# Parts of four units' w_in blocks made in the second block from kept 32-bit values, instead of stored in the first

## The chip, the cores and the metric

The kernel runs on one NeuronCore of one Trainium2 chip. The metric is device time in microseconds (us) of one launch. The kernel before took 808.64 us (median of three runs, 805.9 to 810.67).

## What is computed

Chunked attention over 8 batches, 8 heads, 576 positions in chunks of 64, then a feed-forward layer over the 4608 tokens:

```python
out = softmax(q_c @ k_c.T / 8) @ v_c      # in each chunk of 64
x   = out.transpose(0, 2, 1, 3).reshape(4608, 512)
h   = x @ w_in                            # 512 x 2048
g   = h * tanh(softplus(h))
y   = g @ w_out                           # 2048 x 512
```

Results are 32-bit; each factor of the feed-forward products is split into a high part (rounded to the format that TensorE multiplies in one pass) and a low rest, and three products of the parts are added.

## The kernel before

Tokens go in blocks of 512. The first block is multiplied plainly, with w_in loaded, decoded from 64-bit patterns and split on the way. The later blocks use a seven-product scheme for 2 x 2 blocks (as Strassen's), for which w_in's 256 x 256 blocks and sums of them are needed as split operands. `ops_of[u]` is a DRAM tile with seven such operands for each of eight units u (a unit is 256 columns of w_in): slots 0 to 2 are the plain blocks A11, A12, A22, slots 3 to 6 the four sums. Each slot is 256 KB.

**Who fills the slots.** In the first block, `w_hi` (ScalarE, ACT) and `w_lo` (VectorE, DVE) split a block into `wi[u]`; `w_keep(u)` (L177 to L180) then stores slots 0, 1 and 2 from `wi[u]`, by two DMAs of 512 and 256 KB, for all eight units. The exact 32-bit values of every unit are also kept in DRAM in `cs_u` (`w_c`, L146). The sums are built later from these: `s_load` (L191 to L199) brings `cs_u` back into a buffer with 4 blocks x 2 slots x 256 values per partition, whole values in slot 1; `s_adds` (L201 to L211) makes four sums in place on DVE, 128x256 each; `s_hi` (L215, ACT) writes their high parts into slot 0 of all four blocks; `s_lo` (L219, DVE) makes the low rests and issues one 1 MB store to slots 3 to 6 (L222).

**The order.** The first block's order is the string ORDER; `keep`, `s_load`, `s_adds`, `s_hi`, `s_lo` stand in it for units 0 to 3. The second block (m = 1, about 120 to 252 us of the span, then its second phase) runs `unit(1, u)` for u = 0 to 7. A unit has seven products (n = 0 to 6) of six matmuls, each with one operand from DRAM (`load_op`, L837, five operands ahead, five buffers), between which matmuls of the unit before are put (`filled`). `beside(n)` runs after product n - 1 what BUILDS lists for (u, n). A product's PSUM bank is read by ACT or DVE before it is written again: product 3 (`v`) takes the bank of product 1 (`y`), which DVE's add at L862 reads; product 5 adds to the bank of product 4 (`x`), which ACT copies at L964; product 6 adds to the bank of product 3, which DVE adds to `zb` at L862. In units 1, 3, 5 and 7 a group of four attention tiles also passes through DVE and ACT (L324, L336, L345, L391 to L398). Units 4 to 7 have their sums built one unit ahead: adds at (u-1, 2), high at (u-1, 3), low and store at (u-1, 4), the load of the next at (u-1, 7).

**Queues.** All these loads and stores are issued by one queue, SyncE's (SP), in program order. An instruction there that waits holds up what stands behind it. `zb_p` has two buffers; one holds `wst`, then `a_both` (units 1 and 2), then `zb_1_4`, which unit 4 writes first after its product 2.

Of the kernel before, what the change touches and what calls it, by code (L numbers as in the profile page):

```python
# [9 lines left out]
F32 = mybir.dt.float32  # L10
F32R = mybir.dt.float32r
# [4 lines left out]
ALU = mybir.AluOpType  # L16
AX = mybir.AxisListType

P = 128
# [5 lines left out]
def kernel(  # L25
# [22 lines left out]
    nc = tc.nc  # L48
    NT, _, H, D = q.shape
    NF, _, DM = w_out.shape  # L50
# [3 lines left out]
    NU = NF // 2  # L54
# [5 lines left out]
    at = ctx.enter_context(tc.tile_pool(name="at", bufs=3))  # L60
# [14 lines left out]
    zb_p = ctx.enter_context(tc.tile_pool(name="zb", bufs=2))  # L75
# [5 lines left out]
    ops_of = [dram.tile([P, 7, 2, 256], F32, name=f"wa_{u}") for u in range(NU)]  # L81
# [107 lines left out]
    bld = {}  # L189

    def s_load(u):  # L191
        if u >= NU:
            return
        if u == 1:
            both = zb_p.tile([P, 2, 4, 2, 256], F32, name="a_both", tag="z")
            bld[1], bld[2] = both[:, 0], both[:, 1]
        elif u != 2:
            bld[u] = c_p.tile([P, 4, 2, 256], F32, name=f"a_{u}", tag="c")
        nc.sync.dma_start(  # L199
            out=bld[u][:, :, 1], in_=w_c[u].rearrange("p h (a c) -> p (h a) c", a=2)  # L200
        )  # L201
# [11 lines left out]
    def s_hi(u):  # L213
        t = bld[u]
        nc.scalar.copy(out=t[:, :, 0].bitcast(F32R), in_=t[:, :, 1])  # L215

    def s_lo(u):
        t = bld[u]
        nc.vector.tensor_tensor(  # L219
            out=t[:, :, 1].bitcast(F32R), in0=t[:, :, 1], in1=t[:, :, 0], op=ALU.subtract  # L220
        )
        nc.sync.dma_start(out=ops_of[u][:, 3:], in_=t)  # L222


    def t_whole(u):
# [41 lines left out]
    st = {}  # L267
# [290 lines left out]
    fill = []  # L558
# [64 lines left out]
    def run(plan_, key):  # L623
        for step, arg in plan_.get(key, ()):
            step(arg)
# [26 lines left out]
    def open_accumulators():  # L652
# [53 lines left out]
        15, exp 2, bits 15, load 17, gh 10, scale 16, inverse 2, norm 2, T 2, load_qk 3, up  # L706
        12, bits 16, hi 15, mish 11, lo 15, copy 2, gl 10, x 0 0, hi 16, scale 17, x 0 3, x
        0 4, load 18, V 2, raw 2, lo 16, bits 17, mish 12, fill 11, x 0 2, scores 3, up 13,
        max 3, gh 12, gh 11, x 0 5, gl 11, sub 3, keep 6, scale 18, bits 18, hi 17, lo 17,
        gl 12, hi 18, up 14, lo 18, exp 3, x 0 1, load_v 3, mish 13, mish 14, x 0 6, fill  # L710
        12, inverse 3, keep 5, norm 3, fill 13, keep 7, gh 13, gl 13, up 15, fill 14, s_load
        0, s_adds 0, T 3, s_load 1, ops 2, x 0 8, mish 15, gh 14, gl 14, s_hi 0, copy 3,
        keep 4, s_lo 0, s_adds 1, fl 0, gh 15, s_load 2, ops 3, x 1 0, x 0 7, gl 15, fl 1,
        at 0, x 1 1, V 3, raw 3, x 1 3, fill 15, x 1 4, x 1 2, x 1 5, at 1, x 0 9, x 1 9, x
        1 7, load_qk 4, fl 2, fl 3, x 1 8, s_hi 1, fl 4, at 2, fl 5, fl 6, at 3, x 1 6, s_lo
        1, x 0 10, x 1 10, at 4, s_load 3, at 5, fl 7, st 0, at 6, at 7, st 1, at 8, at 9,
        s_adds 2, s_hi 2, at 10, at 11, s_adds 3, s_lo 2, at 12, at 13, at 14, s_hi 3, s_lo
        3, at 15, at 16, at 17, at 18, at 19, at 20, at 21, at 22, at 23
    """

    BY_SCALAR = (2, 4, 6, 7, 8, 10, 12, 13, 14,)
# [1 line left out]
    def atom(name, *args):  # L723
# [11 lines left out]
        elif name in attention:  # L735
            attention[name](j)
        elif name == "up":
            up(a, last="w")
        elif name == "gh":
            g_upper(it[a], it[a]["z"], f"0_{a}", a in BY_SCALAR)  # L740
        elif name == "gl":
            g_lower(it[a], it[a]["z"], f"0_{a}")
        elif name == "fill":
            if a < NF - 1:
                filled()
            down(0, a, it[a])
        elif name == "fl":
            filled(3)
        elif name == "st":
            for t in (2 * a, 2 * a + 1):  # L750
                store("0", (0, 1), t)
        elif name == "mish":
            it[a]["z"] = z_tile(f"z_{a}")
            mish(it[a]["z"], it[a]["h"])
        elif name == "keep":
            w_keep(a)
        elif name == "x":
            x_step(1, *args)
        elif name == "ops":
            for _ in range(a):  # L760
                load_op()
        else:
            {"s_load": s_load, "s_adds": s_adds, "s_hi": s_hi, "s_lo": s_lo}[name](a)
# [19 lines left out]
    def first_block():  # L783
# [35 lines left out]
    ops = [  # L819
        (m, ops_of, u, OPS.index(n)) for m in range(1, BOTH_FROM) for u in range(NU) for n, _ in PRODUCTS  # L820
    ]
# [40 lines left out]
        nc.vector.tensor_tensor(out=z, in0=o, in1=z, op=ALU.add)  # L862

    zb = {}
    S_STEPS = (s_adds, s_adds, s_hi, s_lo, s_load)
    S_PLACES = (2, 2, 3, 4, 7)
    BUILDS = {(2, 7): [(s_load, 4)]}
    for u in range(4, NU):
        for n, (step, place) in enumerate(zip(S_STEPS, S_PLACES)):
            if n:  # L870
                BUILDS.setdefault((u - 1, place), []).append((step, u + n // 4))


    T_STEPS = (t_whole, t_sums, t_hi, t_lo)
# [20 lines left out]
    def unit(m, u):  # L895
# [8 lines left out]
        def beside(n):  # L904
            if m == 1:
                run(BUILDS, (u, n))
                for key in later.get(8 * u + n, ()):
# [520 lines left out]
```

## Time and profile before

| | |
|---|---|
| median of three runs | 808.64 us (805.9 to 810.67) |
| the profiled execution | 804.22 us, of it the span 802.4 us |
| TensorE (PE) busy in the span | 787.6 us |
| DVE, ACT busy | 547.5 us, 462.6 us |
| DMA moved | 196.12 MB, mean 244 GB/s |

The span runs from the first to the last instruction of the program on the core; the views below are all of this one execution. A wait is named by the engine that waited and by what ended it. A load's landing is when its data and its semaphore have arrived.

### The profile page before, as it was taken

The numbers are of one execution on the slowest core, as the hardware profiler recorded it, in microseconds if no ns is written. First come the engines' busy times: TensorE is split into PE (matmuls) and PEld (weight loads), VectorE is DVE, ScalarE is ACT, GpSimd is POOL, SyncE is SP. The second block draws the span as 40 slices with busy tenths as digits, with TensorE's granted clock in tenths as the row PEclk, the third lists the DMA queues.
The fourth block names the chain that finished last, engine by engine and source line by source line (L and its number), as shares of the span: only waits on it lengthen the run. The fifth ranks groups of instructions, "written<-read, shape, count | busy, mean of one in ns | idle before, by whom it ended". The sixth has DMA issues, their size and how long they took to land.

```text
span 802.4 us, 16472 instructions
## 1 busy us (share of the span) xinstructions
PE 787.6 (98%) x6394; PEld 680.7 (85%) x6394; DVE 547.5 (68%) x835; ACT 462.6 (58%) x694; POOL 0.7 (0%) x6
## 2 busy tenths in 40 slices
PE   4999999999999999999999999999999999999998
PEld 4888787788888888888999998888999988888887
DVE  6789898655656786676688945545698723338875
ACT  5998976534436445566655737566556434455443
POOL 0000000000000000000000000000000000000000
PEclk9999999999999999999999999999999999999999
DMA  9999989877685879988667797776676776766774
GB/s 339 310 327 346 344 290 303 296 229 275 199 296 165 292 249 284 344 297 268 180 179 214 208 279 241 246 253 199 173 209 184 235 219 194 193 195 187 214 193 130
DMA packets 101581, 196.12 MB, mean 244 GB/s; under 512 B 10112, under 2 KB 26496, under 8 KB 99456
## 3 DMA queue, kind: packets, MB, share of 16 engines
q1 hardware_dynamic: 100896, 194.29, 76.2%
q8 instruction: 51, 0.84, 0.4%
q10 hardware_dynamic: 608, 0.79, 0.3%
q14 instruction: 26, 0.21, 0.1%
HBM read 152.04 MB, written 42.99 MB: 243 GB/s over the span
## 4 chain that ended last, share of the span: by engine, by line
PE 96%; DVE 1%; DMA 1%; ACT 1%; issue 0%; ACTq 0%; DVEq 0%
PE x L850 22%; PE X L1279 12%; PE v L850 11%; PE Z L1279 6%; PE y L850 6%; PE o L565 6%; PE h L527 5%; PE Y L1279 3%; PE X_a L1231 3%; PE X L1231 3%; PE Z L1231 3%; PE av L298 2%; PE s L298 2%; PE pt L409 2%; PE Y L1231 1%; PE o_(1, 1)_0_2789 L565 1%
## 5 line engine op out<-in xcount | busy, mean ns | idle before, releaser
L1184 ACT CAST gh<-g 128x512 fp32r<-128x512 f32 x168 | 103.5, 621 | 93.1 <-PE X L1279 29.9
L1187 DVE TENSOR_TENSOR gl<-g,gh 128x512 fp32r<-128x512 f32 x168 | 115.2, 689 | 49.0 <-ACT gh L1184 45.3
L850 PE MATMUL x<-x_T,w 128*128 128x512 f32 x390 | 97.3, 391 | 0.0
L850 PEld LDWEIGHTS x<-x_T,w 128*128 128x128 f32 x390 | 72.6, 188 | 15.4 <-ACT zb L964 0.4
L862 DVE TENSOR_TENSOR g<-v,g 128x512 f32<-128x512 f32 x48 | 33.0, 690 | 73.2 <-ACT g L1162 41.9
L540 ACT ACTIVATE g<-g 128x512 f32<-128x512 f32 x72 | 44.9, 631 | 59.2 <-DVE g L862 58.9
L527 PE MATMUL h<-x_first,wi 128*128 128x512 f32 (+1 forms) x216 | 47.4, 371 | 1.1 <-ACT x_first L449 0.7
L850 PE MATMUL x<-x_T,late 128*128 128x512 f32 x186 | 46.0, 391 | 0.0
L527 PEld LDWEIGHTS h<-x_first,wi 128*128 128x128 f32 x216 | 36.8, 188 | 8.2 <-ACT x_first L449 0.8
L850 PEld LDWEIGHTS x<-x_T,late 128*128 128x128 f32 x186 | 34.6, 188 | 7.0
L1279 PE MATMUL X<-w,gh 128*128 128x256 f32 x288 | 40.5, 283 | 0.0
L565 PE MATMUL o<-wo,gh 128*128 128x512 f32 x128 | 39.5, 390 | 0.0
L1279 PEld LDWEIGHTS X<-w,gh 128*128 128x128 f32 x288 | 37.2, 192 | 0.1
L862 DVE TENSOR_TENSOR g<-y,g 128x512 f32<-128x512 f32 x24 | 16.3, 680 | 30.2 <-PE y L850 29.6
L1162 ACT COPY g<-x 128x512 f32<-128x512 f32 x24 | 14.1, 589 | 37.2 <-PE x L850 37.2
L850 PE MATMUL v<-x_B,w 128*128 128x512 f32 x138 | 35.3, 395 | 0.1
L850 PE MATMUL y<-x_B,w 128*128 128x512 f32 x126 | 31.8, 395 | 0.0
L850 PE MATMUL x<-x_B,w 128*128 128x512 f32 x126 | 31.6, 393 | 0.0
L1279 PE MATMUL X<-late,gh 128*128 128x256 f32 x224 | 31.5, 283 | 0.0
L850 PEld LDWEIGHTS v<-x_B,w 128*128 128x128 f32 x138 | 25.4, 188 | 6.2 <-DVE zb L862 1.0
L850 PE MATMUL v<-x_T,w 128*128 128x512 f32 x120 | 29.6, 390 | 0.0
L1279 PEld LDWEIGHTS X<-late,gh 128*128 128x128 f32 x224 | 28.9, 192 | 0.1
(217 smaller groups left out, 1736.0 us busy)
## 6 DMA issues: line engine op xcount, KB each, us to landing
w<-wa SPq DMA_DIRECT2D x150, 256.0 KB, 3.8
w<-wb SPq DMA_DIRECT2D x94, 256.0 KB, 2.9
late<-wa SPq DMA_DIRECT2D x74, 256.0 KB, 3.1
late<-wb SPq DMA_DIRECT2D x74, 256.0 KB, 2.9
wst<-in_w_in SPq DMA_DIRECT2D x16, 512.0 KB, 5.7
wst<-in_w_out SPq DMA_DIRECT2D x16, 512.0 KB, 6.0
v<-in_v SPq DMA_DIRECT2D x16, 512.0 KB, 6.4
wa<-a SPq DMA_DIRECT2D x6, 1024.0 KB, 4.4
```

The lines of the kernel that those rows point to most:

```text
L298: nc.tensor.matmul(o[h * CHUNK : (h + 1) * CHUNK, c, t - ts.start, g], lhsT=l[rows, t, 2 * g + h], rhs=r[rows, t, 2 * g + h], start=True, ...
L409: nc.tensor.transpose(out=d["pt", ts.start][:, t - ts.start, g], in_=d["p"][:, t, g].rearrange("p c k -> p (c k)"), identity=ident,)
L527: nc.tensor.matmul(h[:, cols], lhsT=wi[i // 2][:, i % 2 * 2 + kt // 2, w_, kt % 2], rhs=x[:, x_, kt, cols], start=(n == 0), stop=(n == 3 * ...
L540: nc.scalar.activation(out=out_, in_=in_, func=AF.Mish)
L565: nc.tensor.matmul(acc[t], lhsT=g[:, t * P : (t + 1) * P], rhs=wo[f // 2][:, f % 2, part], start=(f == 0 and n == 0), stop=(f == NF - 1 an ...
L850: nc.tensor.matmul(o, lhsT=t[:, w_, kt], rhs=x[x_][:, kt], start=(start and i == 0), stop=(i == 5), skip_group_check=not start,)
L862: nc.vector.tensor_tensor(out=z, in0=o, in1=z, op=ALU.add)
L1162: nc.scalar.copy(out=z["G22"], in_=o)
L1184: nc.scalar.copy(out=d["gh"], in_=g)
L1187: nc.vector.tensor_tensor(out=d["gl"], in0=g, in1=d["gh"].bitcast(F32), op=ALU.subtract)
L1231: nc.tensor.matmul(o, lhsT=d[g][:, t * P : (t + 1) * P], rhs=w__, start=(first and n == 2), stop=(u == NU - 1 and g == "gl"), skip_group_c ...
L1279: nc.tensor.matmul(o, lhsT=d[g][:, t * P : (t + 1) * P], rhs=w_[:, part], start=(k in (0, 1, 3) and u == 0 and t % 2 == 0 and n == 0), sto ...
```

## The change

`w_keep` is dropped for units 4 to 7 (eight DMAs, 3 MB). Slots 0 to 2 of these units are made in the second block from the values that `s_load` brings back: `kept_hi` and `kept_lo` split blocks 0 and 1 (128x512) and then block 3 (128x256), with the high and low parts put side by side in slot 0 of the buffer, and store them by two DMAs and one DMA of 256 KB. Then `s_adds`, `s_hi` and `s_lo` run as before on the same buffer; `s_hi` overwrites slot 0. Units 5 and 6 get a buffer of `zb_p` between them, and the places are a table of numbers 8u + n.

```diff
@@ s_load
-        if u == 1:
-            both = zb_p.tile([P, 2, 4, 2, 256], F32, name="a_both", tag="z")
-            bld[1], bld[2] = both[:, 0], both[:, 1]
-        elif u != 2:
+        if u in (1, 5):
+            both = zb_p.tile([P, 2, 4, 2, 256], F32, name=f"a_both_{u}", tag="z")
+            bld[u], bld[u + 1] = both[:, 0], both[:, 1]
+        elif u not in (2, 6):
             bld[u] = c_p.tile([P, 4, 2, 256], F32, name=f"a_{u}", tag="c")
...
+    def kept_slots(u, which):
+        t = bld[u]
+        if which:
+            return t[:, 3, 1], t[:, 0, 0], t[:, 1, 0]
+        return t[:, 0:2, 1], t[:, 0:2, 0], t[:, 2:4, 0]
+
+    def kept_hi(u, which):
+        whole, hi, _ = kept_slots(u, which)
+        nc.scalar.copy(out=hi.bitcast(F32R), in_=whole)
+
+    def kept_lo(u, which):
+        whole, hi, lo = kept_slots(u, which)
+        nc.vector.tensor_tensor(out=lo.bitcast(F32R), in0=whole, in1=hi, op=ALU.subtract)
+        t = bld[u][:, :, 0]
+        if which:
+            nc.sync.dma_start(out=ops_of[u][:, 2], in_=t[:, 0:2])
+        else:
+            for n in range(2):
+                nc.sync.dma_start(out=ops_of[u][:, n], in_=t[:, n::2])
...
@@ ORDER
-        max 3, gh 12, gh 11, x 0 5, gl 11, sub 3, keep 6, scale 18, bits 18, hi 17, lo 17,
+        max 3, gh 12, gh 11, x 0 5, gl 11, sub 3, scale 18, bits 18, hi 17, lo 17, gl 12, hi
...
-    S_STEPS = (s_adds, s_adds, s_hi, s_lo, s_load)
-    S_PLACES = (2, 2, 3, 4, 7)
-    BUILDS = {(2, 7): [(s_load, 4)]}
-    for u in range(4, NU):
-        for n, (step, place) in enumerate(zip(S_STEPS, S_PLACES)):
-            if n:
-                BUILDS.setdefault((u - 1, place), []).append((step, u + n // 4))
+    S_STEPS = (
+        s_load,
+        lambda u: (kept_hi(u, 0), kept_lo(u, 0)),
+        lambda u: (kept_hi(u, 1), kept_lo(u, 1)),
+        s_adds,
+        lambda u: (s_hi(u), s_lo(u)),
+    )
+    S_PLACES = {
+        4: (17, 21, 23, 24, 25),
+        5: (14, 19, 22, 27, 28),
+        6: (15, 26, 29, 30, 31),
+        7: (29, 33, 36, 40, 41),
+    }
+    BUILDS = {}
+    for u, places in S_PLACES.items():
+        for n, step in zip(places, S_STEPS):
+            BUILDS.setdefault((n // 8, n % 8), []).append((step, u))
```

In ORDER, `keep 6`, `keep 5`, `keep 7` and `keep 4` are left out and nothing else moves. PE's order is unchanged. Three places show the rest. Line numbers up to the new functions are those of before; L232, L236, L239, L242 are the new functions', and lines behind are 20 to 30 higher (L862 is L882, L837 is L857, L964 is L994).

VectorE, unit 3 up to its reciprocal, before; `a_4` is unit 4's buffer, `z_1_6<-y_1_3` the add that frees product 3's bank:

```order
L862 TENSOR_TENSOR zb_1_0_1435<-v_1_2_1872,zb_1_0_1435 128x512
L862 TENSOR_TENSOR z_1_6_1934<-y_1_3_1983,z_1_6_1934 128x512
L324 TENSOR_REDUCE m_7_0_1999<-s_7_0_1948 128x16
L336 TENSOR_TENSOR p_7_2001<-s_7_0_1948,m_7_0_1999 128x2x8x64
L211 TENSOR_TENSOR a_4_1932<-a_4_1932 128x256 x4
L551 CAST gh_1_6_2035<-z_1_6_1934 128x512
L555 TENSOR_TENSOR gl_1_6_2037<-z_1_6_1934,gh_1_6_2035 128x512
L391 TENSOR_REDUCE r_7_0_2039<-p_7_2001 128x8x2
```

The same stretch of VectorE now:

```order
L882 TENSOR_TENSOR zb_1_0_1427<-v_1_2_1873,zb_1_0_1427 128x512
L236 TENSOR_TENSOR a_4_1799<-a_4_1799 128x256
L211 TENSOR_TENSOR a_4_1799<-a_4_1799 128x256 x4
L219 TENSOR_TENSOR a_4_1799<-a_4_1799 128x4x256
L882 TENSOR_TENSOR z_1_6_1943<-y_1_3_1999,z_1_6_1943 128x512
L344 TENSOR_REDUCE m_7_0_2015<-s_7_0_1961 128x16
L356 TENSOR_TENSOR p_7_2017<-s_7_0_1961,m_7_0_2015 128x2x8x64
L236 TENSOR_TENSOR a_both_5_1751<-a_both_5_1751 128x2x256
L211 TENSOR_TENSOR a_both_5_1751<-a_both_5_1751 128x256 x4
L571 CAST gh_1_6_2054<-z_1_6_1943 128x512
L575 TENSOR_TENSOR gl_1_6_2056<-z_1_6_1943,gh_1_6_2054 128x512
L411 TENSOR_REDUCE r_7_0_2058<-p_7_2017 128x8x2
```

Unit 4's whole build (its third kept block, four adds, the low rests) stands ahead of the add that frees product 3's bank, and unit 5's first steps behind it.

ScalarE at the same place before, with the semaphores that each waits for:

```order
L924 COPY z_1_6_1934<-x_1_3_1935 128x512 [waits PE_49,Activation_49]
L540 ACTIVATE z_1_6_1934<-z_1_6_1934 128x512 [waits DVE_49]
L948 COPY zb_1_0_1435<-x_1_3_1935 128x512 [waits PE_49]
L345 ACT_TABLE_LOAD [waits DMAHW0_49]
L345 ACTIVATE p_7_2001<-p_7_2001 128x1024 [waits DVE_49]
L215 CAST a_4_1932<-a_4_1932 128x4x256 [waits DMAHW7_49,DMAHW4_49,DVE_49]
L964 COPY zb_1_0_1435<-x_1_3_1935 128x512 [waits PE_49]
```

ScalarE there now, with the semaphores that each waits for (DMAHW is a DMA's landing); L215 is `s_hi`:

```order
L232 CAST a_4_1799<-a_4_1799 128x256 [waits DMAHW2_49,Activation_49]
L954 COPY z_1_6_1943<-x_1_3_1948 128x512 [waits PE_49]
L215 CAST a_4_1799<-a_4_1799 128x4x256 [waits DMAHW3_49,DMAHW7_49,DVE_49,Activation_49]
L560 ACTIVATE z_1_6_1943<-z_1_6_1943 128x512 [waits DVE_49]
L232 CAST a_both_5_1751<-a_both_5_1751 128x2x256
L978 COPY zb_1_0_1427<-x_1_3_1948 128x512 [waits PE_49]
L365 ACT_TABLE_LOAD [waits DMAHW4_49]
L365 ACTIVATE p_7_2017<-p_7_2017 128x1024 [waits DVE_49]
L215 CAST a_both_5_1751<-a_both_5_1751 128x4x256 [waits DMAHW5_49,DVE_49]
L994 COPY zb_1_0_1427<-x_1_3_1948 128x512 [waits PE_49]
```

The L215 of `a_4` moved ahead of L345, right behind the copy of product 0's bank; in its old place stands unit 5's.

SyncE's queue at the end of unit 1 and in unit 2, before:

```order
L837 DMA w16_1738<-wa_2_110 128x512
L837 DMA w17_1755<-wa_2_110 128x512
L222 DMA wa_3_111<-a_3_1559 128x2048
L837 DMA w18_1768<-wa_2_110 128x512
L837 DMA w19_1798<-wa_2_110 128x512
L837 DMA w20_1811<-wa_2_110 128x512
L281 DMA q_7_1855<-in_q 128x2x512
L281 DMA k_7_1856<-in_k 128x2x512
L837 DMA w21_1865<-wa_3_111 128x512
```

The same stretch of the queue now; w16 to w22 are operands of products (2, 2) to (3, 1):

```order
L857 DMA w16_1730<-wa_2_110 128x512
L857 DMA w17_1747<-wa_2_110 128x512
L199 DMA a_both_5_1751<-cs_5_129 128x4x256
L222 DMA wa_3_111<-a_3_1551 128x2048
L857 DMA w18_1762<-wa_2_110 128x512
L199 DMA a_both_5_1751<-cs_6_130 128x4x256
L857 DMA w19_1793<-wa_2_110 128x512
L199 DMA a_4_1799<-cs_4_128 128x4x256
L857 DMA w20_1808<-wa_2_110 128x512
L301 DMA q_7_1852<-in_q 128x2x512
L301 DMA k_7_1853<-in_k 128x2x512
L857 DMA w21_1862<-wa_3_111 128x512
```

The three L199 rows are new here; before, unit 4's stood behind w25, and those of units 5 and 6 in units 3 and 4. Behind w21 now follow two kept stores (L242), w22, w23 and two more.

## Rows read from the trace of the kernel before

**Rows 1.** The page, part 1: busy time, share of the span, instructions.

```profile
span 802.4 us, 16472 instructions
PE 787.6 (98%) x6394; PEld 680.7 (85%) x6394; DVE 547.5 (68%) x835; ACT 462.6 (58%) x694; POOL 0.7 (0%) x6
```

**Rows 2.** Waits of PE, first and last of seven: total, times, longest.

```profile
PE s L298 <- DMA k<-in_k: 5.1, 2, 4.9
...
PE s L298 <- issue: 0.2, 1, 0.2
```

**Rows 3.** Windows: length, busy PE, PEld, DVE, ACT, POOL, clock, DMA share, GB/s.

```profile
23.57:150.00 126.43, 126.08 (x1109) 102.97 (x1109) 112.04 (x148) 105.33 (x130) 0.00 (x0) 1.00 0.92 320
150.00:800.00 650.00, 648.78 (x4998) 567.32 (x4996) 418.27 (x654) 342.80 (x541) 0.00 (x0) 1.00 0.74 227
```

**Rows 4.** The chain that ended last, in order of time: start, length, what.

```profile
143.95 4.89 DMA w<-wa
```

**Rows 5.** Windows, columns as in rows 3: units 2, 3, 4 of the second block.

```profile
151.91:168.28 16.37, 16.37 (x133) 13.42 (x132) 4.11 (x7) 6.07 (x9) 0.00 (x0) 1.00 0.80 271
168.28:185.43 17.15, 17.15 (x139) 14.00 (x138) 12.25 (x20) 8.61 (x11) 0.00 (x0) 1.00 0.62 206
185.43:201.81 16.38, 16.38 (x133) 13.43 (x132) 6.57 (x11) 7.13 (x10) 0.00 (x0) 1.00 0.79 274
```

**Rows 6.** Line L837 at 156.1 and 159.4 us: issue of w20, w21, their landing.

```profile
L837 SPq DMA_DIRECT2D w<-wa x1: 1207/1207/1207, 156.1 to 156.1; - x1
DMA to landing us min/median/max: 6.8/6.8/6.8
...
L837 SPq DMA_DIRECT2D w<-wa x1: 339/339/339, 159.4 to 159.4; - x1
DMA to landing us min/median/max: 6.7/6.7/6.7
```

**Rows 7.** Timeline of PE: products (2, 6), (3, 0), (3, 3), (3, 5), (3, 6).

```profile
166.25 1.52 PE L850 MATMUL v<-x_B,w 128*128 128x512 f32 x6
...
168.28 1.52 PE L850 MATMUL x<-x_B,w 128*128 128x512 f32 x6
...
176.41 1.52 PE L850 MATMUL v<-x_T,w 128*128 128x512 f32 x6
...
181.16 1.52 PE L850 MATMUL x<-x_T,w 128*128 128x512 f32 x6
...
182.53 1.59 PE L850 MATMUL v<-x_B,w 128*128 128x512 f32 x6
```

**Rows 8.** Timeline of DVE in unit 3: start, length, line, tiles, shape.

```profile
173.27 0.69 DVE L862 TENSOR_TENSOR z<-y,z 128x512 f32<-128x512 f32 x1 [2.97 <-PE y L850]
...
176.27 1.79 DVE L211 TENSOR_TENSOR a<-a 128x256 f32<-128x256 f32 x4
177.98 0.42 DVE L551 CAST gh<-z 128x512 fp32r<-128x512 f32 x1
...
180.67 1.16 DVE L219 TENSOR_TENSOR a<-a 128x1024 fp32r<-128x1024 f32 x1
181.75 0.68 DVE L862 TENSOR_TENSOR zb<-v,zb 128x512 f32<-128x512 f32 x1
```

**Rows 9.** Timeline of ACT in unit 3, columns as in rows 8.

```profile
170.34 0.63 ACT L540 ACTIVATE zb<-zb 128x512 f32<-128x512 f32 x1 [3.24 <-DVE zb L862]
...
178.57 1.04 ACT L215 CAST a<-a 128x1024 fp32r<-128x1024 f32 x1
180.23 0.59 ACT L964 COPY zb<-x 128x512 f32<-128x512 f32 x1 [0.63 <-PE x L850]
```

**Rows 10.** Line L837, 160 to 186 us: nine operand loads, time to landing.

```profile
DMA to landing us min/median/max: 2.6/2.8/5.1
```

**Rows 11.** The page, part 6: all operand loads of this kind, KB, median us to landing.

```profile
w<-wa SPq DMA_DIRECT2D x150, 256.0 KB, 3.8
```

**Rows 12.** Timeline of ACT in unit 4: the first write of `zb_1_4`.

```profile
192.94 0.59 ACT L948 COPY zb<-x 128x512 f32<-128x512 f32 x1 [0.54 <-PE x L850]
```

More of the change, by code (lines that the diff above doesn't have):

```diff
@@ L708 @@
         0 4, load 18, V 2, raw 2, lo 16, bits 17, mish 12, fill 11, x 0 2, scores 3, up 13,
-        max 3, gh 12, gh 11, x 0 5, gl 11, sub 3, keep 6, scale 18, bits 18, hi 17, lo 17,
[L710 to L718, printed above, removed]
+        max 3, gh 12, gh 11, x 0 5, gl 11, sub 3, scale 18, bits 18, hi 17, lo 17, gl 12, hi
+        18, up 14, lo 18, exp 3, x 0 1, load_v 3, mish 13, mish 14, x 0 6, fill 12, inverse
+        3, norm 3, fill 13, gh 13, gl 13, up 15, fill 14, s_load 0, s_adds 0, T 3, s_load 1,
+        ops 2, x 0 8, mish 15, gh 14, gl 14, s_hi 0, copy 3, s_lo 0, s_adds 1, fl 0, gh 15,
+        s_load 2, ops 3, x 1 0, x 0 7, gl 15, fl 1, at 0, x 1 1, V 3, raw 3, x 1 3, fill 15,
+        x 1 4, x 1 2, x 1 5, at 1, x 0 9, x 1 9, x 1 7, load_qk 4, fl 2, fl 3, x 1 8, s_hi
+        1, fl 4, at 2, fl 5, fl 6, at 3, x 1 6, s_lo 1, x 0 10, x 1 10, at 4, s_load 3, at
+        5, fl 7, st 0, at 6, at 7, st 1, at 8, at 9, s_adds 2, s_hi 2, at 10, at 11, s_adds
+        3, s_lo 2, at 12, at 13, at 14, s_hi 3, s_lo 3, at 15, at 16, at 17, at 18, at 19,
+        at 20, at 21, at 22, at 23
     """
```

## Prediction

> **What bounds the kernel.** I read the page first, then who waits for whom, then stretches of the span, then the timelines of the stretch that the change touches. PE is busy 787.6 of 802.4 us [rows 1]. Its seven waits begin with 5.1 us for the first load and end with 0.2 us [rows 2], and the windows show that they lie at the start: from 23.57 to 150 us PE is idle for 0.35 us, from 150 to 800 us for 1.2 us, at full clock (1.00, the level of 2.4 GHz) [rows 3]. So behind the first 23 us there is nothing for another engine to give back. The change adds no matmul and takes none away: the time can fall only by PE's small waits, and it grows by every wait that the change makes. The question is how much room PE's suppliers have where the new work is put, in units 1 to 5.
>
> **What is removed.** Eight stores (3 MB) leave the first block. PE hardly waits there. The tightest operands come after it: the chain shows product (1, 6)'s operand issued at 143.95 us, landed 4.89 us later, and PE starting on it at once [rows 4]. The lighter queue makes such landings earlier; PE gains what it waits there, a tenth or two. I take **-0.1 us** (ends 0 and -0.35, all that PE idles up to 150 us).
>
> **What is added.** Per unit 4 to 7: two splits on ACT and two on DVE, and three stores for two. The eight loads and builds are the same work as before, elsewhere. Two terms reach PE.
>
> **A, late operands in units 2 and 3.** Three `s_load`s of 512 KB now stand in SP's queue between w17 and w20. Around there (unit 2) the DMA engines move 271 GB/s at a share of 0.80 [rows 5], 339 GB/s when busy, so a load takes 1.55 us of them, three 4.65 us. w20 was issued at 156.1, landed 6.8 later, at 162.9, and was used at 166.25; w21 at 159.4 + 6.7 = 166.1, used at 168.28 [rows 6, 7]: room of 3.3 and 2.2 us. What is put in front takes the room and 4.65 - 2.2 = **2.4 us** more. The lower end is 0: at a share of 0.80 the engines idle 3.3 us of unit 2, and with 2.2 us of room that could hide all. The upper end adds the four kept stores that follow directly (256 KB, 0.77 us each, 3.1 us): 5.5 us. I take 2.4, since the idle share lies mostly ahead of these loads, not behind: landings of 6.7 us against a median of 3.8 [rows 11] say that things queue there.
>
> **B, VectorE and ScalarE in unit 3.** In unit 3 DVE is busy for 12.25 of 17.15 us, unit 4's adds and low rests among it [rows 5]. Now come two kept splits of 256 columns (0.45 each, a quarter of the 1.79 us of four such adds), one of 512 (0.69), and units 5's and 6's builds (1.79 + 1.16 each) [rows 8]: 0.9 + 0.7 + 5.9 = 7.5 us, together 19.7 us in a window of 17.15. That alone is 2.6 us too much. Before and after lie units with 4.11 and 6.57 us [rows 5], but an engine works in its order, and PE waits at three points. In the clock of before:
>
> - *B1, product (3, 3).* ACT is free of unit 2 at 170.97 [rows 9]. The high part of the kept block of 256 takes 0.4 (by the 512 and 1024 columns of [rows 9]), the low rest 0.45: stored at 171.8. Now `s_hi` of unit 4 overwrites what that store reads, so ACT waits for its landing. With the fastest, 2.6 us [rows 10], it starts at 174.4; it takes 1.04 [rows 9], `s_lo` 1.16 behind it, and only then comes the add of `y`, 0.69 [rows 8]: done at 177.3, not 173.96. Product (3, 3) writes that bank and started at 176.41 [rows 7]: 0.9 us late.
> - *B2, product (3, 5).* From that add's end to the end of four adds DVE took 178.06 - 173.96 = 4.1 us [rows 8]; with the kept 0.69 it is 4.8: 182.1. ACT's `s_hi` of unit 5 waits for these adds (1.04), and the copy of product 4's bank stands behind it (0.59): 183.7. Product (3, 5) would start at 181.16 + 0.9 = 182.1 [rows 7]: 1.6 us late.
> - *B3, product (3, 6).* From the adds' end to the end of the add on product 3's bank DVE took 4.4 us (178.06 to 182.43) [rows 8]: 186.5. Product (3, 6) would start at 182.53 + 0.9 + 1.6 = 185.0 [rows 7]: 1.5 us late.
>
> Together 4.0 us with the fastest landing. Nothing later binds: the next `y` add falls into unit 4, where DVE is idle for 9.8 us. But the store lands behind others; every us goes into B1. Nine operand loads around there took 2.6 to 5.1, median 2.8, [rows 10], all of that kind 3.8 [rows 11]. As A's loads and the other stores now stand there, I take 3.8: **B = 4.0 + 1.2 = 5.2 us**; ends 2.6 (the surplus of work alone) and 6.5 (landing at 5.1).
>
> The Trainium skill, "DMA: Bandwidth & Descriptors", section "Anatomy of one DMA — SWDGE (gpsimd) path", gives a fixed 2.0 us plus bytes at 436 GB/s, most of it the receipt of the write. It is measured on another issuing path; an estimate by that page is 2.6 us for a store of 256 KB, which agrees with the fastest row and has no queue in it. By it B would be 4.0 and the sum 6.3 us. The queue's rows decide for the larger one.
>
> No operand is loaded before it is made: w28, unit 4's first, is issued nine rows behind its store, and those of units 5 to 7 a unit or more behind theirs.
>
> **The sum.** -0.1 + 2.4 + 5.2 = **+7.5 us**. On the profiled execution, 804.22 us, that is 811.7; it lies 4.4 us under the median of the runs, 808.64, so the forecast is **816.1 us** (+0.9%). About 0.5%, 4 us here, is what a measurement of this kernel can tell from no change.
>
> **Rivals.**
> 1. *The cover holds.* For: DVE is idle for 12 us in unit 2 and 9.8 us in unit 4, DMA has 3 MB less to do just before, and B adds up durations one by one where neighbours on an engine may overlap. Against: the order fixes who waits, and ACT's wait for a store is there however free the queue is. It takes a store landed in 2.6 us and idle DMA engines, A = 0, B at or under 2.6: 808.6 to 811.2, about **810**. Chance 0.28.
> 2. *Faster.* The runs lie 4.4 us over the profiled execution. Should this be waits in units 0 and 1, where operands land just in time [rows 4], the lighter first block takes them away: -4.4 us. If the cover also holds: **804.2**. It decides when landings there are some 0.5 us later in other executions than in this one. Against: any cause common to the whole span explains the 4.4 us as well. Chance 0.05.
> 3. *Worse, by a late buffer.* `zb_1_4` takes the buffer of units 5 and 6, whose last low rests follow unit 3's last add, some 4 us before unit 4's product 2; ACT's first write to it, at 192.94 [rows 12], now waits for that landing. From a landing of about 6 us on, as in [rows 6], PE waits too, by some 2 us. With A at 4 and B at 6.5: +12.4, **821.0**. Chance 0.17.
>
> The forecast itself has 0.50.
>
> **How the numbers follow.** Under the forecast the time goes from +4.0 (A 0, B 4.0) to +9; under rival 3 to +12.4; under rival 1 it is +0 to +2.6. The range 808.0 to 821.0 leaves out rival 2 and the outer ends. Slower by over 0.5%: 0.50 and 0.17 less the few cases under +4 us, 0.65. Faster: rival 2 alone, 0.05. The same: 0.30.
>
> **What would show it.** Right: PE idle or its products stretched by about 5 us in unit 3 (168 to 195 us) with ACT, DVE named as releasers of `v` and `x`; L215 on ACT waiting for a DMA from the buffer; PE waits of 1 to 3 us for w20 to w22; DVE busy for nearly all of unit 3; span 809 to 811. The first block and everything behind unit 5 should keep their length. Wrong: unit 3 still 17.2 us long with PE never waiting (B fails), operands w20 and w21 landing as before (A fails), or a shift ahead of 150 us.

## The result and the profile after

The changed kernel takes **816.79 us** (median of five runs, 815.49 to 820.52), the kernel before 807.04 (five runs, the three from above among them): ratio 1.0118, 95% interval 1.0096 to 1.014, so 9.5 us slower, 7.7 to 11.3. The forecast was 816.1. The profiled execution is the 816.79 us one, with a span of 815.0 us against the 802.4 of [rows 1]. Of the lines not named above, L850 is now L870 (product), L924 and L948 are L954 and L978 (two of ScalarE's copies), L540 is L560 (activation).

The windows of units 2, 3 and 4 of the second block say where the time went. Each begins with its first product; columns as in rows 3:

```profile
154.56:174.16 19.60, 17.05 (x134) 13.12 (x132) 5.65 (x10) 7.10 (x11) 0.00 (x0) 1.00 0.95 307
174.16:196.63 22.47, 18.15 (x138) 13.92 (x139) 17.73 (x31) 11.08 (x16) 0.00 (x0) 1.00 0.81 268
196.63:214.26 17.63, 16.71 (x133) 13.20 (x132) 6.57 (x11) 7.87 (x12) 0.00 (x0) 1.00 0.91 313
```

Against [rows 5] unit 2 has grown by 3.23 us (16.37 before), unit 3 by 5.32 (17.15) and unit 4 by 1.25 (16.38): 9.8 us, close to the measured difference of 9.5. Unit 2 starts 2.65 us later than in the trace before (154.56 for 151.91); experiment e1, which takes no longer than before, starts it 4.06 us later, so this is not put down to the change. From unit 5 on the shift stays as it is to 0.2 us.

The waits of PE, in us in total, times, longest, hold rows that [rows 2] does not have:

```profile
PE s L318 <- DMA k<-in_k: 5.3, 1, 5.3
...
PE x L870 <- DMA w<-wa: 2.6, 2, 2.0
PE v L870 <- DVE z L882: 1.9, 1, 1.9
PE x L870 <- ACT zb L994: 1.2, 1, 1.2
PE v L870 <- DVE zb L882: 1.1, 1, 1.1
PE x L870 <- ACT zb L978: 0.9, 1, 0.9
```

PE's timeline gives each its product: (2, 4), (3, 0), (3, 3), (3, 5), (3, 6) and (4, 4), with the idle time before it in brackets:

```profile
165.79 1.62 PE L870 MATMUL x<-x_T,w 128*128 128x512 f32 x6 [0.53 <-DMA w<-wa]
...
174.16 1.63 PE L870 MATMUL x<-x_B,w 128*128 128x512 f32 x6 [2.03 <-DMA w<-wa]
...
184.59 1.66 PE L870 MATMUL v<-x_T,w 128*128 128x512 f32 x6 [1.90 <-DVE z L882]
...
190.86 1.66 PE L870 MATMUL x<-x_T,w 128*128 128x512 f32 x6 [1.21 <-ACT zb L994]
...
193.66 1.66 PE L870 MATMUL v<-x_B,w 128*128 128x512 f32 x6 [1.14 <-DVE zb L882]
...
208.22 1.65 PE L870 MATMUL x<-x_T,w 128*128 128x512 f32 x6 [0.92 <-ACT zb L978]
```

The first two are term A (the operand of (2, 4) is w18, that of (3, 0) is w21), the next three term B, at the three products that the prediction names. The last one is the place of rival 3.

**Behind A** stands something that the prediction does not have. SP's timeline (start, length of the issue):

```profile
155.98 0.57 SPq L222 DMA_DIRECT2D wa<-a  x1
156.64 0.38 SPq L857 DMA_DIRECT2D w<-wa  x1
157.07 0.64 SPq L199 DMA_DIRECT2D a_both<-cs  x1
157.76 1.99 SPq L857 DMA_DIRECT2D w<-wa  x1
163.85 0.53 SPq L199 DMA_DIRECT2D a<-cs  x1
164.48 0.56 SPq L857 DMA_DIRECT2D w<-wa  x1
...
166.08 0.46 SPq L857 DMA_DIRECT2D w<-wa  x1
```

From 159.75 to 163.85 us SP issues nothing: 4.1 us. What it stands at is L199, unit 4's load, by SP's waits (total, times, longest):

```profile
SPq L199 <- DMA wa<-a: 4.0, 1, 4.0
```

Its buffer is the one of unit 3 (`c_p` has one), and unit 3's store, issued at 155.98, still reads that; it landed 7.8 us later, at 163.8. Behind the load in the same queue stand w20 (164.48, landed at 169.67, used at 169.80) and w21 (166.08, landed 7.9 us later, at 174.02, used at 174.16). In the trace before they were issued at 156.1 and 159.4 [rows 6]. The 0.53 us of (2, 4) are not the pause's: w18 was issued ahead of it, at 156.64, and landed 9.0 us later.

**Behind B**, ScalarE's timeline:

```profile
174.78 0.41 ACT L232 CAST a_both<-a_both 128x256 fp32r<-128x256 f32 x1 [4.22 <-DMA wa<-a_both]
...
181.63 1.05 ACT L215 CAST a<-a 128x1024 fp32r<-128x1024 f32 x1 [2.60 <-DMA wa<-a]
...
189.27 1.05 ACT L215 CAST a_both<-a_both 128x1024 fp32r<-128x1024 f32 x1 [0.70 <-DVE a_both L211]
190.23 0.58 ACT L994 COPY zb<-x 128x512 f32<-128x512 f32 x1
...
207.58 0.59 ACT L978 COPY zb<-x 128x512 f32<-128x512 f32 x1 [2.47 <-DMA wa<-a_both]
```

L215 is `s_hi` of unit 4; it waits for the kept store issued at 179.02, which landed 2.5 us later. L232 at 174.78 is the second kept split of unit 5: it overwrites the slots that the first split's two stores still read, and those, issued at 166.64 and 167.07 behind the loads, took 8.1 and 8.3 us. L978 is the first write of `zb_1_4` into the buffer of units 5 and 6. VectorE's timeline:

```profile
175.48 0.42 DVE L236 TENSOR_TENSOR a_both<-a_both 128x256 fp32r<-128x256 f32 x1 [4.83 <-DMA wa<-a_both]
...
176.89 0.68 DVE L882 TENSOR_TENSOR zb<-v,zb 128x512 f32<-128x512 f32 x1
...
182.71 1.23 DVE L219 TENSOR_TENSOR a<-a 128x1024 fp32r<-128x1024 f32 x1 [1.88 <-ACT a L215]
183.85 0.68 DVE L882 TENSOR_TENSOR z<-y,z 128x512 f32<-128x512 f32 x1
...
187.44 1.79 DVE L211 TENSOR_TENSOR a_both<-a_both 128x256 f32<-128x256 f32 x4
...
192.93 0.68 DVE L882 TENSOR_TENSOR zb<-v,zb 128x512 f32<-128x512 f32 x1
```

The add of `y` (183.85) stands behind `s_lo` (182.71), and product (3, 3) starts when it ends. The copy at 190.23 stands behind `s_hi` of unit 5 (189.27), and product (3, 5) starts when it ends. From 182.71 to 198.6 VectorE runs without a gap.

### The profile page after: what moved, and what is told of

Read it like the earlier page. It is cut to its first block, busy times and chain, and to the rows that moved or that the text cites. A ratio compares the mean times of both kernels' runs of the same rounds, so it can differ in the third digit from the quotient of the medians.

```text
span 815.0 us, 16490 instructions
## 1 busy us (share of the span) xinstructions
PE 790.9 (97%) x6394; PEld 679.9 (83%) x6394; DVE 551.4 (68%) x843; ACT 466.1 (57%) x702; POOL 0.7 (0%) x6
## 4 chain that ended last, share of the span: by engine, by line
PE 76%; DMA 9%; DVE 8%; ACT 4%; issue 2%; SPq 1%; ACTq 0%; DVEq 0%
PE x L870 19%; PE X L1309 11%; PE v L870 10%; PE Z L1309 6%; PE y L870 5%; PE Y L1309 3%; PE X_a L1261 3%; PE X L1261 3%; PE Z L1261 3%; DMA wst<-in_w_in 2%; DMA wa<-a 2%; DMA wst<-in_w_out 2%; DVE wc L142 2%; DMA q<-in_q 1%; PE Y L1261 1%
## 5 line engine op out<-in xcount | busy, mean ns | idle before, releaser
L870 PE MATMUL x<-x_T,w 128*128 128x512 f32 x390 | 97.7, 392 | 2.7 <-ACT zb L994 1.2
L870 PEld LDWEIGHTS x<-x_T,w 128*128 128x128 f32 x390 | 72.4, 188 | 19.1 <-ACT zb L994 2.1
L882 DVE TENSOR_TENSOR g<-v,g 128x512 f32<-128x512 f32 x48 | 33.0, 690 | 73.4 <-ACT g L1192 42.1
L560 ACT ACTIVATE g<-g 128x512 f32<-128x512 f32 x72 | 44.9, 631 | 59.6 <-DVE g L882 59.3
L870 PE MATMUL x<-x_T,late 128*128 128x512 f32 x186 | 46.0, 391 | 0.0
L870 PEld LDWEIGHTS x<-x_T,late 128*128 128x128 f32 x186 | 34.6, 188 | 7.0
L882 DVE TENSOR_TENSOR g<-y,g 128x512 f32<-128x512 f32 x24 | 16.3, 680 | 30.7 <-PE y L870 30.0
L870 PE MATMUL v<-x_B,w 128*128 128x512 f32 x138 | 35.3, 395 | 1.1 <-DVE zb L882 1.1
L870 PE MATMUL x<-x_B,w 128*128 128x512 f32 x126 | 31.8, 394 | 2.0 <-DMA w<-wa 2.0
L870 PE MATMUL v<-x_T,w 128*128 128x512 f32 x120 | 29.9, 392 | 2.7 <-DVE z L882 1.9
L870 PE MATMUL y<-x_B,w 128*128 128x512 f32 x126 | 31.9, 396 | 0.1
L870 PEld LDWEIGHTS v<-x_B,w 128*128 128x128 f32 x138 | 25.4, 188 | 7.3 <-DVE zb L882 1.6
L870 PEld LDWEIGHTS v<-x_T,w 128*128 128x128 f32 x120 | 22.3, 188 | 8.4 <-DVE z L882 2.9
```

Of the source, the lines that this page charges most:

```text
L560: nc.scalar.activation(out=out_, in_=in_, func=AF.Mish)
L870: nc.tensor.matmul(o, lhsT=t[:, w_, kt], rhs=x[x_][:, kt], start=(start and i == 0), stop=(i == 5), skip_group_check=not start,)
```

## The experiments

Each kernel was timed in five rounds beside the kernel before. The lengths of the units are read from each profiled execution, from first product to first product:

| | ratio, 95% interval | start of unit 2 | unit 2 | unit 3 | unit 4 |
|---|---|---|---|---|---|
| before | 1 | 151.91 | 16.37 | 17.15 | 16.38 |
| after | 1.0118, 1.0096 to 1.014 | 154.56 | 19.60 | 22.47 | 17.63 |
| e1_no_keeps | 0.9995, 0.9985 to 1.0006 | 155.97 | 16.38 | 17.16 | 16.38 |
| e2_places | 1.0046, 1.0028 to 1.0064 | 156.15 | 18.63 | 18.72 | 17.75 |
| e3_no_stores | 1.0079, 1.0063 to 1.0096 | 154.94 | 18.10 | 19.04 | 17.53 |
| e4_late_hi | 1.0108, 1.0089 to 1.0127 | 155.97 | 19.89 | 20.59 | 18.82 |
| e5_load6 | 1.0056, 1.0029 to 1.0083 | 154.56 | 18.83 | 17.20 | 17.63 |
| e7_load4 | 1.0031, 1.0017 to 1.0045 | 157.49 | 16.89 | 17.70 | 17.40 |
| e8_early6 | 1.0051, 1.0031 to 1.0071 | 156.65 | 20.51 | 17.23 | 16.37 |
| e9_mended | 1.0076, 1.0054 to 1.0099 | 154.87 | 16.82 | 20.72 | 18.29 |
| e10_both | 1.0018, 0.9999 to 1.0037 | 154.15 | 16.83 | 17.74 | 16.38 |
| e11_no_lo | 1.0101, 1.007 to 1.0133 | 153.26 | 19.64 | 22.19 | 17.38 |

The theory is the prediction's sum. Its rivals: that the first block's lighter queue gives time back, and that some of the cost is not work and bytes but an engine or a queue that stands and waits.

**e1_no_keeps: the removal alone.** The kernel before, with `keep 4` to `keep 7` taken out of `ORDER`, and units 4 to 7 reading slots 0 to 2 of units 0 to 3.

```diff
-... sub 3, keep 6, scale 18, ... inverse 3, keep 5, norm 3, fill 13, keep 7, gh 13, ... copy 3, keep 4, s_lo 0
+... sub 3, scale 18, ... inverse 3, norm 3, fill 13, gh 13, ... copy 3, s_lo 0
-            nc.sync.dma_start(out=t.bitcast(F32), in_=src[u][:, place])
+            nc.sync.dma_start(out=t.bitcast(F32), in_=src[u - 4 if place < 3 and u > 3 and src is ops_of else u][:, place])
```

> The kernel before without the eight stores of units 4 to 7 in the first block; the loads of these units' slots 0 to 2 in the second block read units 0 to 3 instead, so the plain blocks of units 4 to 7 are left out of the result. It prices the removal alone. Theory (PE has nothing to gain or lose in the first block): the same as before to within 0.5 us, ratio 0.999 to 1.001, all of unit 2 to 4 as before. Rival (the 1.3 us by which the changed kernel falls behind between 92 and 149 us come from the missing stores): 1.3 us slower, ratio 1.0016. Rival (the time over the profiled execution sits in late operands of units 0 and 1): 4 us faster, 0.995.

807.58 against 808.12 us: eight stores of 3 MB less, and no time. Units 2 to 4 keep their length to 0.01 us. And though nothing was added, unit 2 starts 4.06 us later than in the trace before; the rows are of the kind that the prediction's second rival names, at the last products of units 0 and 1:

```profile
135.11 1.63 PE L850 MATMUL v<-x_B,w 128*128 128x512 f32 x6 [1.69 <-DMA w<-wa]
...
153.02 1.63 PE L850 MATMUL v<-x_B,w 128*128 128x512 f32 x6 [1.13 <-DMA w<-wa]
```

So the waits ahead of unit 2 differ from execution to execution. Of the twelve profiled executions in the table the one of before starts unit 2 earliest (151.91; the others 153.26 to 157.49), which goes well with its 4.4 us under the median. Fewer stores in the first block do not cure it.

**e2_places: the places, loads and buffers alone.** The changed kernel with the kept parts stored in the first block again and no kept splits.

```diff
-        lambda u: (kept_hi(u, 0), kept_lo(u, 0)),
-        lambda u: (kept_hi(u, 1), kept_lo(u, 1)),
+        lambda u: None,
+        lambda u: None,
```

> The changed kernel with the eight stores back in the first block and without the kept splits and their stores: what is left of the change is the new places of the loads, the adds, the high and low parts, and the buffers. It computes the reference. Theory (late operands in units 2 and 3 come from the three loads; the waits in unit 3 come from the stores that are overwritten and from the added splits): 2.6 us over before, ratio 1.003, PE waiting for w before (2, 4) to (3, 0) by 2 to 3 us and by under 1 us for ACT and DVE in unit 3. Rival (DVE's crowded unit 3 alone makes those waits): 6 us over before, ratio 1.007, with the waits of (3, 3), (3, 5), (3, 6) still there. Rival (the late operands come from the kept stores in the queue): under 0.5 us over before.

811.7 us, +3.7 (0.46%). The theory had 2.6, with nothing in unit 4. Unit 2 is 2.26 us longer and unit 4 1.37. Unit 3's 1.57 us are the clock, told of at the end, and no wait.

**e3_no_stores: the kept splits too, but not their stores.** The first block stores the kept parts.

```diff
-        t = bld[u][:, :, 0]
-        if which:
-            nc.sync.dma_start(out=ops_of[u][:, 2], in_=t[:, 0:2])
-        else:
-            for n in range(2):
-                nc.sync.dma_start(out=ops_of[u][:, n], in_=t[:, n::2])
```

> The changed kernel with the eight stores back in the first block, and with the kept splits on ACT and DVE but without their twelve stores. It computes the reference (the splits' results go nowhere). Theory: no landing is waited for before the high parts, so (3, 3) starts in time; the crowded DVE still delays (3, 5) and (3, 6), by about 2 us together, and the loads cost 2.6: 4.5 us over before, ratio 1.0055. Rival (all of the waits in unit 3 are landings): 2.6 us over before, 1.003. Rival (all are the added work): 7.5 us and more, 1.009.

814.46 us, +6.4 by the ratio where the theory had 4.5; e2's surplus of 1.1 is part of that. Product (3, 3) is in time again, since `s_hi` of unit 4 now waits for work only:

```profile
177.10 1.05 ACT L215 CAST a<-a 128x1024 fp32r<-128x1024 f32 x1 [1.81 <-DVE a L211]
```

What is left in unit 3 is above all 1.14 us at (3, 6), behind VectorE. By the ratios the places cost 0.46%, the splits 0.33% and the stores with the waits for their landing 0.39% of the time: 3.7, 2.7 and 3.1 us, each to about 2 us.

**e4_late_hi: unit 4's high and low parts three products later.**

```diff
-        4: (17, 21, 23, 24, 25),
+        4: (17, 21, 23, 24, 28),
```

> The changed kernel with one number other: unit 4's high and low parts at (3, 4) and not (3, 1), three products later than the store that they overwrite. Theory: ACT waits for no landing there, the wait of 1.9 us before (3, 3) goes; but the same work comes in front of (3, 5) and (3, 6), which grow by 0.5: 1.4 us under the changed kernel, ratio to before 1.010. Rival (the landing is not the cause): as the changed kernel, 1.012, with the wait before (3, 3) still over 1.5 us.

The wait of (3, 3) is gone. The edit takes the landing, `s_hi` and `s_lo` from ahead of it together; that it was the landing and not the work is shown by e3, which keeps the work there. But (3, 6) now waits 2.1 us, as VectorE has both units' `s_lo` ahead of the add, and more operands are late. Unit 3 is 1.9 us shorter, units 2 and 4 together 1.5 longer: 816.4 us, no difference to after.

**e5_load6 and e7_load4: which of two causes has A.** Both start from e2.

```diff
e5_load6
-        6: (15, 26, 29, 30, 31),
+        6: (22, 26, 29, 30, 31),
e7_load4
-        4: (17, 21, 23, 24, 25),
+        4: (19, 21, 23, 24, 25),
```

> Edit: e2 (new places, loads and buffers; kept parts stored in the first block) with unit 6's load at 22 instead of 15, so that two 1 MB loads stand in the stretch of 154 to 166 us where there were three. e2 measured 1.0046 of before, and its profile shows about 2 us of TensorE waits for w<-wa there. Theory of the prediction (the loads take the operands' bandwidth, 1.55 us each): one load less gives back its 1.55 us, ratio about 1.003, the two waits for w<-wa under 1 us together. Rival (SP stands at unit 4's load, which reuses the buffer that unit 3's store still reads, and the operands behind it are issued about 4 us late): that store is issued ahead of unit 6's load and so lands at most some 0.5 us earlier; SP still pauses over 3 us, ratio 1.004 to 1.005.

> Edit: e2 with unit 4's load at 19 instead of 17, so that it comes up in SP's queue after unit 3's store has landed (163.8 us in the profile of after) and after two more operands. All three loads stay. Rival of e5's text (SP's pause is what delays the operands): no pause of over 3 us in SP's queue between 159 and 166 us, the two operands are issued 4 us earlier, the waits for w<-wa of e2 (2.0 us in its profile) go, ratio 1.002 to 1.003. Theory of the prediction (bandwidth): the same bytes move within the same products, the waits are moved by a product or two and stay at 2 us, ratio 1.0046.

(The expectations call the loads 1 MB; they are 512 KB, as the prediction has it.) e5 takes a third of the loads' bytes out of the stretch, and unit 2 keeps its length (18.83 us, 18.63 in e2). SP still stands, now 6.0 us, from 158.12 to 164.12:

```profile
156.16 0.57 SPq L222 DMA_DIRECT2D wa<-a  x1
156.82 1.30 SPq L857 DMA_DIRECT2D w<-wa  x2
164.12 0.58 SPq L199 DMA_DIRECT2D a<-cs  x1
```

e7 keeps all three loads and moves one of them behind two more operands. The longest pause of SP between 159 and 167 us is now 0.8 us, and the operand of (3, 0) is issued at 165.28, 7.8 us after unit 2's start (168.09 and 11.9 us in e2):

```profile
161.71 2.34 SPq L857 DMA_DIRECT2D w<-wa  x2
164.10 0.49 SPq L301 DMA_DIRECT2D q<-in_q  x1
164.70 0.48 SPq L301 DMA_DIRECT2D k<-in_k  x1
165.28 0.41 SPq L857 DMA_DIRECT2D w<-wa  x1
166.50 0.54 SPq L199 DMA_DIRECT2D a<-cs  x1
```

Unit 2 is 16.89 us long, 0.5 over before. The waits of products into `x` for operands, 2.0 us in e2, are down to 0.5:

```profile
PE x L870 <- DMA w<-wa: 0.5, 2, 0.3
```

In e5 and in e7 two of the three loads stand ahead of w20 and w21 (those of units 5 and 4 in e5, of 5 and 6 in e7), all of one size; what differs is the pause. So A is the queue that stands, with about 0.5 us for the bytes of two loads. The times alone do not settle it (the intervals of e2, e5 and e7 overlap); the lengths of unit 2 and the pauses do, and all traces agree: in the seven with unit 4's load at 17 (after, e2 to e5, e8, e11) SP waits there for unit 3's store for 3.1 to 6.0 us and unit 2 is 18.10 to 20.51 us long; in the three with it at 19 (e7, e9, e10) both operands stand ahead of it and unit 2 is 16.82 to 16.89 us long. A buffer of its own for unit 4's load was not tried.

**e8_early6: units 5 and 6 finished earlier.** From e2:

```diff
-        5: (14, 19, 22, 27, 28),
-        6: (15, 26, 29, 30, 31),
+        5: (14, 19, 22, 20, 21),
+        6: (15, 26, 29, 27, 28),
```

> Edit: e2 with units 5 and 6 finished earlier: unit 5's sums at 20 and its split at 21 (27 and 28 before), unit 6's at 27 and 28 (30 and 31 before). If the wait of about 1 us in unit 4 (ScalarE's first write to zb_1_4, which takes the buffer of units 5 and 6) is the landing of the last store from that buffer, it goes: the store is issued about 6 us earlier, ratio about 1.0034. If it is something else (the copy is late for another reason), it stays at 1 us, ratio 1.0046.

The wait in unit 4 is gone, and unit 4 is back at 16.37 us: it was the late buffer. The time does not show it (1.0051, 1.0046 in e2, with intervals that overlap). In the profiled execution unit 2 takes back more than the gain, its operands being later still: (2, 6) and (3, 0) wait 1.05 and 2.64 us. For the second the profile names ScalarE:

```profile
177.16 1.63 PE L870 MATMUL x<-x_B,w 128*128 128x512 f32 x6 [2.64 <-ACT zb L560]
```

But the operand, issued at 169.09, landed 7.9 us later, 0.14 us before the product began, as far ahead as w21 in after (174.02, 174.16). SP's pause is there as in e2; why it costs more here is open.

**e10_both: both cures.** e2 with the edits of e7 and e8.

> Edit: e2 with the edits of e7 and e8 together (unit 4's load at 19; unit 5's sums and split at 20 and 21, unit 6's at 27 and 28). If the 3.7 us that e2 takes over before are SP's pause (about 2.5 us) and the buffer of units 5 and 6 that comes free late (about 1 us), both go: no waits for w<-wa of over 0.5 us in units 2 and 3, none at the copy into zb_1_4, ratio 1.000 to 1.002. If the bytes of three loads, or the two buffers themselves, cost something of their own, it stays over 1.003.

810.07 against 809.17 us: no change that the interval shows. Units 2 and 3 are 0.46 and 0.59 us longer than before, unit 4 not at all, and the waits left there are

```profile
PE x L870 <- DMA w<-wa: 0.3, 1, 0.3
PE v L870 <- DVE zb L882: 0.3, 1, 0.3
```

The buffer for units 5 and 6 and the early loads thus cost little in themselves (0.18%, 1.5 us, with 3 us at the upper end); their places in the queue did.

**e11_no_lo: VectorE's part of B.** The changed kernel without the low halves of the kept parts of units 4 and 6.

```diff
-        nc.vector.tensor_tensor(out=lo.bitcast(F32R), in0=whole, in1=hi, op=ALU.subtract)
+        if u % 2:
+            nc.vector.tensor_tensor(out=lo.bitcast(F32R), in0=whole, in1=hi, op=ALU.subtract)
...
-                nc.sync.dma_start(out=ops_of[u][:, n], in_=t[:, n::2])
+                nc.sync.dma_start(out=ops_of[u][:, n], in_=t[:, n::2] if u % 2 else t[:, 0:2])
```

> Edit: the changed kernel without VectorE's subtractions for the kept parts of units 4 and 6 (the low halves of those operands are left out, their high halves are stored twice instead); ScalarE's copies, all places and all stores stay. VectorE has 0.42 us less ahead of product (3,3) and 0.68 us less ahead of (3,5). If VectorE's row of work without a gap sets the waits of (3,3), (3,5) and (3,6) (1.9, 1.2 and 1.1 us in the profile of after), they come to about 1 us less together, ratio 1.010 to 1.011. If ScalarE's copies or the landing of the stores set them, the three stay at 4.2 us together, ratio 1.0115 to 1.012.

The wait of (3, 5) is gone and that of (3, 6) halved; (3, 3) still waits (lines have moved by one, L883 is the add):

```profile
PE v L871 <- DVE z L883: 2.2, 1, 2.2
...
PE v L871 <- DVE zb L883: 0.5, 1, 0.5
```

Part of that is PE's own lateness, since the clock fell behind the wait of (3, 3); see the end. What tells more is the way from (3, 3) to (3, 6), both of which start when an add on VectorE ends: 193.66 - 184.59 = 9.07 us in after, 192.12 - 183.66 = 8.46 here. It is 0.61 us shorter, with 0.68 us of VectorE's work left out on it, though PE was slower. So VectorE's row of work sets (3, 6). (3, 3) is set by the landing: ScalarE's `s_hi` stood 2.93 us for it, which took 3.3 us from the issue at 177.31. The ratio fits, but its interval holds after's as well.

**e9_mended: the best version of the changed kernel that was found.**

```diff
-        4: (17, 21, 23, 24, 25),
+        4: (19, 22, 24, 25, 28),
-        6: (15, 26, 29, 30, 31),
+        6: (22, 26, 29, 30, 31),
```

> Edit: the changed kernel with unit 4's steps at 19, 22, 24, 25, 28 instead of 17, 21, 23, 24, 25 and unit 6's load at 22 instead of 15. If the parts found so far add up, the operands' waits in units 2 and 3 go (-2 us), the wait of product (3,3) goes (-1.9 us) with about 1 us more at (3,6) as in e4, and the wait in unit 4 stays: about -3 us on after, 812.5 to 814 us, ratio 1.006 to 1.008. If the later load of unit 4 makes ScalarE wait for it at its first split (in order, with the copies of unit 3 behind it), the gain is taken back: ratio 1.010 to 1.012. No version of this order is expected at or under the kernel before, since VectorE's added time in unit 3 stays.

813.52 us, as the first case of the expectation has it. The operand waits named in units 2 and 3 are down to 0.16 us and (3, 3) starts in time; (3, 5) waits 1.6 us, (3, 6) 1.2 and (4, 4) 1.2. Unit 3 is still 3.6 us over before. No version ran faster than the kernel before.

## Why the prediction was right, and where it was not

**The total** was +7.5 us, measured 9.5 (7.7 to 11.3); 816.1 against 816.79 us. That the two times lie so close is in part luck: the forecast started from 808.64 us, and the kernel before took 807.04. By parts, from the windows: A 3.2 for 2.4, B 5.3 for 5.2, unit 4 1.25 for nothing.

**What bounds the kernel** held. PE had nothing to give back, and e1 shows that 3 MB less in the first block are worth 0 (0.9985 to 1.0006), as the -0.1 said. The second rival had its place right, waits in units 0 and 1, and its cause wrong: they come and go between executions with or without the stores.

**A: size near by luck, cause wrong.** The step that failed is "What is put in front takes the room and 4.65 - 2.2". It counts bytes. For two loads ahead of w20 and w21 the same sum gives 3.1 - 2.2 = 0.9 us. e7 has two there and no pause over 0.8 us: unit 2 is 0.5 us longer. e5 has two there and the pause: 2.46 us. Three loads there without the pause were not run. I had looked for what is queued in front of w20, and not for what the instruction ahead of it in SP's queue waits for. The pause makes w20 and w21 be issued 5.7 and 4.0 us late beyond the shift of unit 2's start, against 3.3 and 2.2 us of room; that unit 3's store and unit 4's load share a buffer stood in the code.

**B1: right sum by luck, two errors that cancel.** `s_hi` waits for the landing, `s_lo` and the add of `y` behind it, and PE's shift against the trace before grows from 5.88 us at (3, 0) to 8.18 at (3, 3): 2.3 us, for 2.1 worked out. But the landing took 2.5 us, near the fastest of the nine [rows 10] and not the 3.8 I chose (3.3 in e11). Instead the store was issued late. PE's shift at (3, 0) is 5.9 us, so 171.8 becomes 177.7; it went out at 179.02. The reason is the wait of VectorE at 175.48 for the landing of unit 5's first kept stores. Behind it in order stands the add at 176.89, which is 1.4 us late beyond PE's shift of 5.88, then ScalarE's mish, then the split. In the trace before it was

```profile
169.62 0.68 DVE L862 TENSOR_TENSOR zb<-v,zb 128x512 f32<-128x512 f32 x1
```

The prediction had not seen that the second kept split overwrites what the first one's stores read. The Trainium skill, "DMA: Bandwidth & Descriptors", section "Anatomy of one DMA — SWDGE (gpsimd) path", by which the prediction estimated 2.6 us, agrees with the 2.5 us of the store at 179.02; the two stores of 256 KB that went out behind loads took 8.1 and 8.3, for which the 6.8 and 6.7 us of operands in the queue [rows 6] were the nearer guide.

**B2 and B3** came as 1.5 and 1.4 us of shift (9.70 us at (3, 5), 11.13 at (3, 6)) for 1.6 and 1.5 worked out. From the end of the add of `y` to the end of the four adds went 4.7 us for 4.8, from there to the end of the add on product 3's bank 4.4 for 4.4. Their mechanism, VectorE's work in its order, has e11's 0.61 us for it. The 19.7 us of VectorE's work in unit 3, from which the lower end of 2.6 came, were too many: 17.73 were measured, and unit 6's low rests, counted among them, ran at 201.12 us, in unit 4.

**"Nothing later binds" failed.** Product (4, 4) waits 0.92 us. That is rival 3's mechanism at half its price; the landing of the last store from the buffer of units 5 and 6 came 5.1 us after its issue at 202.37 and 2.47 us after ScalarE was ready. e8 and e10 take it away. It should have been in the sum with a small price rather than in a rival with the rest at its upper end.

**What would show it**: named right were PE's waits in unit 3 and their releasers, L215's wait for a DMA, and the wait of 1 to 3 us for the operand of (3, 0). Not so were waits for w20 and w22, which were in time, and VectorE busy for nearly all of unit 3 (17.73 of 22.47 us). Wrong was the span, 809 to 811: it is 815.0, and 2.65 us of the difference lie ahead of unit 2. That shift is one of the prediction's signs of being wrong; e1 has it too, so executions differ there. A forecast of a profile carries that spread too.

## What to carry to other kernels

Cost a moved load first by the buffer that it takes: if the last reader is a store still under way, the queue stands until that has landed, and everything behind it is late by the pause, however few bytes the load has. The same holds for each step that overwrites what a store reads, on every engine and in every reused slot: list the pairs of store and overwriter, and give each store time to land at the latency that it has behind the transfers queued there. Before a row of one profiled execution is taken as the place of a gain, see whether the same row comes and goes in other executions.

## What the runs showed of the hardware that was not expected

**Half the clock behind a short wait, twice.** In e2 PE waited 1.83 us at (3, 0), and the nine matmuls of 512 columns behind it took 3.71 us; in the trace before they took 2.14 (168.28 to 170.42). Windows of the trace before, and of e2 ahead of, in and behind the stretch (length, PE, PEld, DVE, ACT, POOL, granted clock, DMA share, GB/s):

```profile
168.28:170.42 2.14, 2.14 (x11) 1.51 (x9) 1.72 (x3) 0.08 (x1) 0.00 (x0) 1.00 0.74 227
...
172.00:174.78 2.78, 0.95 (x5) 0.45 (x4) 1.69 (x4) 0.00 (x0) 0.00 (x0) 1.00 1.03 379
174.78:178.49 3.71, 3.71 (x10) 2.44 (x10) 1.64 (x5) 1.76 (x3) 0.00 (x0) 0.56 0.40 138
178.49:181.00 2.51, 2.51 (x71) 2.23 (x71) 1.23 (x1) 0.41 (x1) 0.00 (x0) 0.96 0.88 308
```

A granted clock of 0.56 is the lower level, 1.2 GHz, for nearly all of the 3.71 us. It cost 1.57 us beside the wait itself. In e11 the same happened behind the wait of 2.22 us at (3, 3), at 0.54. After's own waits of 2.03 and 1.90 us, e4's of 2.21 and e8's of 2.64 were followed by matmuls at the full clock (1.00). So a wait of about 2 us may be paid nearly twice or not, and part of the spread between runs of these kernels may be that; what decides between the two was not tried.

**Landings of 8 to 10 us.** Behind two loads of 512 KB and a store of 1 MB in SP's queue, an operand of 256 KB issued at 157.76 us landed 9.9 us later (3.8 is the median of its kind in both profiles), and the engines' share was 0.95 in unit 2.
